# Keys projected and exponentiated two tiles ahead of their sums, with six feature buffers, in the first stage of a fused attention and mixture kernel

## Chip, core and metric

The kernel runs on one core of one Trainium2 chip. The metric is the device time of one execution in microseconds (us), the median of several runs. Five engines work side by side, each through a queue of its own in order: TensorE (PE, with its weight loads as PEld), VectorE (DVE), ScalarE (ACT), GpSimd (POOL) and SyncE (SP), which issues the DMA transfers.

## The reference

Three layers follow one another on 4 x 576 = 2304 tokens. The change touches the first, a linear attention with 8 heads of 64 and 128 random features:

```python
def phi(x):
    proj = np.einsum('bhsd,df->bhsf', x, w_phi)
    proj = proj - np.max(np.abs(proj), axis=-1, keepdims=True)
    return np.concatenate([np.exp(proj), np.exp(-proj)], axis=-1)
q_p, k_p = (phi(q), phi(k))
kv = np.einsum('bhsf,bhsd->bhfd', k_p, v)
z = np.sum(k_p, axis=2)
num = np.einsum('bhsf,bhfd->bhsd', q_p, kv)
den = np.einsum('bhsf,bhf->bhs', q_p, z)[..., None] + 1e-06
return (num / den).astype(np.float32)
```

Its result goes, as 2304 x 512, into a gated layer (RMS norm, then gate, value and output matrices with 1536 hidden units) and from there into a soft mixture of 8 experts. Everything is float32.

## The kernel before

There are three stages. The **first stage** goes over the keys in 18 tiles of 128 tokens. For each tile `Front.load` fetches the keys (256 KB) and `K.load_v` the values. `project` multiplies the keys by `w_phi` into two PSUM banks, one for the even and one for the odd heads ("hf" 0 and 1); the two halves of PE's rows take one each, four matmuls a bank, each seen as two instructions in the trace, so 8 + 8. `largest` and `less`, together `shift`, take the largest magnitude and subtract it (DVE). `exps` writes exp(x) and exp(-x) of a half into a buffer `kp` (ACT, two instructions a half). `kv` adds both halves into the sums of the batch entry on PE: `kv_of` (L439, 8 instructions a half) and `z_of` (L448, 8 a half). A batch entry ends every 4.5 tiles; then `Evac` copies its sums out and `Evac.turn` transposes them.

In iteration i of the loop the program writes: project and shift of tile i + 1, `kv` of tile i, `exps` of tile i + 1, and between these the other work of the stage. That is the conversion of nine pieces of the gated layer's weights (`conv_load`, `conv_scale`, `conv_join`, `conv_parts`: DMA, ACT, DVE, then ACT and POOL), the transposes of the sums (`fillers`) and the queries of the first 384 tokens in steps (`qsteps`, made by `Turned.steps` at the places in `TURNED0`: project, transpose and exponentiate, `attend` per pair of heads at steps 12, 15, 20 and 26 of 36, then `scale` and `out`).

The written order is not the order on an engine. A planner lays out each queue ahead of the run: among the instructions whose inputs and buffers it reckons ready, it takes the one that stands first in the program. Buffers with one tag go round: `kp` has four of 4 KB a partition, the keys' raw tiles four, `pr` (the shifted projections) three halves, the PSUM banks `P` two.

The **second stage** is the gated layer in six blocks of 384 tokens, with the conversion of the other nine weight pieces in its first block (two raw buffers, loaded from the block's start on); its SBUF tiles lie over those of the first stage and wait for them. The **third stage** is the expert matrices, loaded by DMA.

Of the kernel before, what the change touches and what calls it, by code (L numbers as in the profile page):

```python
# [7 lines left out]
F32 = mybir.dt.float32  # L8
# [8 lines left out]
NB, NH, SEQ, HD, DF = 4, 8, 576, 64, 128  # L17
# [3 lines left out]
TILES = NT // 128  # L21
# [19 lines left out]
def batch_parts(i):  # L41

    t0, parts = i * 128, []
    r = 0
    while r < 128:
        b = (t0 + r) // SEQ
        end = min(128, (b + 1) * SEQ - t0)
        parts.append((b, r, end))
        r = end
    return parts  # L50
# [14 lines left out]
def tile_kernel(ctx: ExitStack, tc: tile.TileContext, q2T, qT, kT, v, wbd, wg, wv, wo, rmsg, phi, w1, w2, consts, out):  # L65
# [3 lines left out]
    def pool(stack, name, space=None, bufs=1, side="left"):  # L69
        kw = {} if space is None else {"space": space}  # L70
        if space is None:
            kw["side"] = side
        if space is not DRAM:
            kw["reuse_waits"] = "tile"
        return stack.enter_context(tc.tile_pool(name=name, bufs=bufs, **kw))
# [73 lines left out]
    def conv_load(sp, bufs, *pools):  # L149

        key = next(conv_at, None)
        if key is not None:
            c = Conv(sp, pools[pieces.index(key) % len(pools)], key, bufs)
            c.load()
            loaded.append(c)

    def conv_scale():
        if loaded:
            convs.append(loaded.pop(0))
            convs[-1].scale()  # L160

    def conv_join():
        if convs:
            convs[-1].join()
            if convs[-1].n == 2:
                joined.append(convs.pop())

    def conv_parts():
        if joined:
            joined.pop(0).parts()  # L170
# [85 lines left out]
    class Reduced(Q):  # L256
# [25 lines left out]
        def exps(self, h):  # L282
            e = self.e[h]
            DVE.tensor_tensor(out=e[:, 1], in0=e[:, 1], in1=e[:, 0], op=ALU.subtract)
            ACT.activation(out=e[:, 0], in_=e[:, 1], func=AF.Exp)
            ACT.activation(out=e[:, 1], in_=e[:, 1], func=AF.Exp, scale=-1.0)
# [83 lines left out]
    with ExitStack() as pk:  # L370
        kx = pool(pk, "kx")
        sp = pool(pk, "spk")
# [35 lines left out]
        class K(Front):  # L408
# [2 lines left out]
                SP.dma_start(out=self.vt, in_=v[self.i].rearrange("p (h d) -> p h d", h=NH))  # L411

            def exps(self, hf):
                kp = sp.tile([128, 4, 2, DF], F32, tag="kp", name="kp", bufs=4)
                ACT.activation(out=kp[:, :, 0], in_=self.pr[hf], func=AF.Exp)
                ACT.activation(out=kp[:, :, 1], in_=self.pr[hf], func=AF.Exp, scale=-1.0)  # L416
                self.e[hf] = kp
# [75 lines left out]
        ks = [K(sp, psk, kT, i, kb if i else dict(kb, P=("misc", 3))) for i in range(TILES)]  # L493
# [13 lines left out]
        for _ in range(2):  # L507
            conv_load(sp, KCONV, sp)
        conv_scale()
        ks[0].project()  # L510
        for hf in range(2):
            ks[0].shift(hf)
            ks[0].exps(hf)
        fillers = []
        q0 = Turned(sp, psk, 0, {"misc": 3, "raw": 2, "pr": 3, "e": 2})
        qsteps = q0.steps(TURNED0[0:4], TURNED0[4:8], TURNED0[8:])
        qsteps = [[f for m, f in qsteps if m == n] for n in range(2 * TILES)]
        q0.begin()
        for i in range(TILES):
            k, kn = ks[i], ks[i + 1] if i + 1 < TILES else None  # L520
            if i + 3 < TILES:
                ks[i + 3].load()
            if i + 2 < TILES:
                ks[i + 2].load_v()
            if i % 2 and i // 2 + 2 < NPRE:
                conv_load(sp, KCONV, sp)
            parts = batch_parts(i)
            b = parts[0][0]
            ends = i * 128 + parts[0][2] == (b + 1) * SEQ

            def finish():
                ev = Evac(b)
                fillers.extend([lambda n=n: ev.turn(n) for n in range(3)])

            if len(parts) > 1:
                k.kv(parts[0])
                finish()
            if kn:
                kn.project()
                kn.shift(0)  # L540
                kn.largest(1)
                conv_join()
                kn.less(1)
            k.kv(parts[-1])
            for hf in range(2):
                if kn:
                    kn.exps(hf)
                if hf == 0 and i % 2:
                    conv_parts()
                    conv_scale()  # L550
                if fillers:
                    fillers.pop(0)()
                for f in qsteps[2 * i + hf]:
                    f()
            if ends and len(parts) == 1:
                finish()
# [47 lines left out]
    with ExitStack() as p2:  # L604
# [5 lines left out]
        sp = pool(tctx, "conv")  # L610
# [233 lines left out]
        for blk in range(NBLK):  # L844
            acc = [ps.tile([128, DM], F32, tag=f"acc{i}", name=f"acc{i}", bufs=1) for i in range(TPB)]
            qsteps, qnext = qnext or [], None
            if blk == 1:
# [6 lines left out]
                sp = pool(pctx, "post", side="right")  # L854
            if blk == NBLK - 1:
# [5 lines left out]
                sp = pool(pctx, "post", side="right")  # L861
# [62 lines left out]
    with ExitStack() as p3:  # L924
        sp = pool(p3, "sp3")
# [145 lines left out]
```

## Time and profile before

| what | value |
|---|---|
| median of 3 runs | 745.16 us (744.03 to 750.23) |
| the profiled execution's own time | 744.73 us |
| its span | 742.9 us |
| mean granted TensorE clock | 0.995 of full |
| PE busy | 713.5 us, 96% of the span |
| ACT, DVE busy | 371.6 us (50%), 428.1 us (58%) |
| first stage, from the span's start to PE's first gate matmul (L804) | 134.2 us |

The time is the execution's, the span is what the trace covers, 1.8 us less. In the trace a row gives start, duration, engine, line, operation and tile; the bracket behind it is the idle time of that engine before the row and what ended it. A busy PE is not PE at its best rate: the spacing of the rows shows how fast the same work goes.

### The profile page before, as it was taken

The page shows a single profiled execution, that of the slowest core. Times are in us where ns is not written, and L with a number is a line of the kernel's source. Part 1 is how long each engine was busy: PE and PEld are TensorE (multiplying, and loading weights), DVE is VectorE, ACT ScalarE, POOL GpSimd, SP SyncE. Part 2 cuts the span into 40 slices and gives each one's busy share as a digit, 9 for nine tenths or more (in the row PEclk, how much of TensorE's full clock was granted, in tenths as well). Part 3 has the DMA queues.
Part 4 walks back from the last instruction along what each step waited for, and adds up shares of the span by engine and source line. Part 5 has one row for each costly group of instructions (what it writes and reads, how often), then busy time and mean ns, then how long its engine had stood idle before and what let it go on. Part 6 is the DMA issues. An engine that isn't in the chain of part 4 may idle for free.

```text
span 742.9 us, 12354 instructions
## 1 busy us (share of the span) xinstructions
PE 713.5 (96%) x4919; PEld 575.1 (77%) x4919; DVE 428.1 (58%) x808; ACT 371.6 (50%) x805; POOL 108.3 (15%) x60
## 2 busy tenths in 40 slices
PE   6999898999899999999999999999999999999894
PEld 4555554888789888898888988889888899988343
DVE  5888956687756646555565555655556453323313
ACT  6689855588644465334654346543465431211103
POOL 0222210135200211012110121101211010000100
PEclk9999999999999999999999999999999999999998
DMA  9674211545010100101000010000100237657898
GB/s 325 225 243 182 72 44 45 187 158 208 8 61 23 33 22 23 49 0 33 22 23 20 1 33 22 23 19 1 33 1 2 65 120 275 228 199 288 318 362 285
DMA packets 25146, 79.47 MB, mean 107 GB/s; under 512 B 2688, under 2 KB 13376, under 8 KB 18688
## 3 DMA queue, kind: packets, MB, share of 16 engines
q1 hardware_dynamic: 24864, 77.79, 30.0%
q10 hardware_dynamic: 224, 0.88, 0.4%
q8 instruction: 39, 0.64, 0.3%
q14 instruction: 19, 0.16, 0.1%
HBM read 71.99 MB, written 6.67 MB: 106 GB/s over the span
## 4 chain that ended last, share of the span: by engine, by line
PE 76%; ACT 10%; DVE 6%; issue 2%; DMA 2%; POOL 1%; SPq 0%; DVEq 0%; ACTq 0%; POOLq 0%
PE pv L804 18%; PE pg L804 17%; PE acc L829 6%; PE acc L830 6%; PE acc L831 6%; PE num L206 4%; PE kacc L439 3%; PE den L214 2%; PE y L943 2%; ACT e L224 2%; PE kacc L448 2%; PE y L959 2%; DVE wt L137 1%; DMA wraw<-in_wg_dram 1%; ACT wt L127 1%
## 5 line engine op out<-in xcount | busy, mean ns | idle before, releaser
L804 PE MATMUL pv<-xnh,wv 128*128 128x384 f32 x576 | 151.6, 344 | 0.0
L804 PE MATMUL pg<-xnh,wg 128*128 128x384 f32 x576 | 150.2, 342 | 1.3 <-DVE t L812 1.0
L804 PEld LDWEIGHTS pg<-xnh,wg 128*128 128x128 f32 x576 | 104.7, 188 | 7.2 <-DVE t L812 1.5
L804 PEld LDWEIGHTS pv<-xnh,wv 128*128 128x128 f32 x576 | 103.2, 188 | 7.0 <-issue 6.7
L804 PE MATMUL pv<-xnl,wv 128*128 128x384 f32 x288 | 97.7, 339 | 0.0
L804 PE MATMUL pg<-xnl,wg 128*128 128x384 f32 x288 | 97.5, 338 | 0.0
L829 PE MATMUL acc<-wo,hh 128*128 128x512 f32 x216 | 88.6, 410 | 0.0
L280 POOL PARTITION_ALL_REDUCE qe<-qe x32 | 50.0, 1563 | 262.7 <-ACT qe L279 243.0
L830 PE MATMUL acc<-wo,hh 128*128 128x512 f32 x216 | 85.9, 397 | 0.0
L831 PE MATMUL acc<-wo,hl 128*128 128x512 f32 x216 | 85.4, 395 | 0.0
L102 ACT CAST hh<-t 128x384 fp32r<-128x384 f32 x72 | 36.7, 509 | 79.8 <-PE acc L830 66.1
L105 DVE TENSOR_TENSOR hl<-t,hh 128x384 fp32r<-128x384 f32 x72 | 41.3, 574 | 52.7 <-ACT hh L102 50.3
L812 DVE SCALAR_TENSOR_TENSOR t<-t,pg 128x384 f32<-128x384 f32 x72 | 39.7, 551 | 51.3 <-ACT t L811 51.2
L811 ACT ACTIVATE t<-pg 128x384 f32<-128x384 f32 x72 | 35.1, 488 | 62.5 <-PE pg L804 62.3
L224 ACT COPY qe<-qe 32x192 f32<-32x192 f32 x128 | 44.8, 350 | 31.7 <-DVE qe L219 30.4
L816 DVE TENSOR_TENSOR t<-t,pv 128x384 f32<-128x384 f32 x72 | 39.8, 552 | 30.2 <-PE pv L804 29.0
L804 PEld LDWEIGHTS pg<-xnl,wg 128*128 128x128 f32 x288 | 54.0, 188 | 0.3 <-DVE xnl L105 0.3
L804 PEld LDWEIGHTS pv<-xnl,wv 128*128 128x128 f32 x288 | 54.1, 188 | 0.1
L439 PE MATMUL kacc<-kp,vt 128*64 128x256 f32 (+1 forms) x320 | 43.8, 399 | 5.3 <-ACT kp L416 5.2
L831 PEld LDWEIGHTS acc<-wo,hl 128*128 128x128 f32 x216 | 40.6, 188 | 10.0 <-DVE hl L105 0.3
L829 PEld LDWEIGHTS acc<-wo,hh 128*128 128x128 f32 x216 | 40.7, 189 | 7.3 <-issue 0.3
L830 PEld LDWEIGHTS acc<-wo,hh 128*128 128x128 f32 x216 | 40.7, 188 | 6.4
(187 smaller groups left out, 1069.2 us busy)
## 6 DMA issues: line engine op xcount, KB each, us to landing
eu<-in_w_dram SPq DMA_DIRECT2D x32, 1024.0 KB, 6.5
wraw<-in_wg_dram SPq DMA_DIRECT2D x6, 1024.0 KB, 5.5
wraw<-in_wv_dram SPq DMA_DIRECT2D x6, 1024.0 KB, 6.6
wraw<-in_wo_dram SPq DMA_DIRECT2D x6, 1024.0 KB, 5.0
qraw<-in_qT_dram SPq DMA_DIRECT2D x32, 192.0 KB, 2.4
raw<-in_kT_dram SPq DMA_DIRECT2D x18, 256.0 KB, 3.5
vt<-in_v_dram SPq DMA_DIRECT2D x18, 256.0 KB, 2.9
out_dram<-ob SPq DMA_DIRECT2D x18, 256.0 KB, 3.4
```

What stands on the lines that cost most here:

```text
L102: ACT.copy(out=hi, in_=src)
L105: (lo_eng or POOL).tensor_tensor(out=lo, in0=src, in1=hi.bitcast(F32), op=ALU.subtract)
L224: ACT.copy(out=rd[64 * hh + 32 * r:64 * hh + 32 * r + 32, g], in_=dn[o:o + 32])
L280: POOL.partition_all_reduce(e[:, 0], e[:, 1], channels=128, reduce_op=bass_isa.ReduceOp.absmax)
L439: PE.matmul(out=kva[o0:o0 + 64, hh // 2], lhsT=self.vt[r0:r1, h], rhs=kp[r0:r1, hh].rearrange("p s f -> p (s f)"), start=first and hh < 2, ...
L804: PE.matmul(out=p, lhsT=w[:, a, c], rhs=x, start=n == 0, stop=n == 11)
L811: ACT.activation(out=t, in_=g, func=AF.Tanh, scale=0.5)
L812: DVE.scalar_tensor_tensor(out=t, in0=t, scalar=1.0, in1=g, op0=ALU.add, op1=ALU.mult)
L816: DVE.tensor_tensor(out=t, in0=t, in1=wide("v", m, xs), op=ALU.mult)
L829: PE.matmul(out=acc[i], lhsT=hh[:, s], rhs=w[:, 0], start=m == 0, stop=False)
L830: PE.matmul(out=acc[i], lhsT=hh[:, s], rhs=w[:, 1], start=False, stop=False)
L831: PE.matmul(out=acc[i], lhsT=hl[:, s], rhs=w[:, 0], start=False, stop=m == MF - 1)
```

## The change

The keys' front (project, shift, exponentiate) now runs two tiles ahead of the sums: tiles 0 and 1 before the loop, and tile i + 2 in iteration i. `kp` gets six buffers instead of four (8 KB more a partition). The keys' raw tiles are asked for four tiles ahead instead of three, tile 3 before the loop; their four buffers stay.

```diff
-                kp = sp.tile([128, 4, 2, DF], F32, tag="kp", name="kp", bufs=4)
+                kp = sp.tile([128, 4, 2, DF], F32, tag="kp", name="kp", bufs=6)
...
         conv_scale()
-        ks[0].project()
-        for hf in range(2):
-            ks[0].shift(hf)
-            ks[0].exps(hf)
+        ks[3].load()
+        for k in ks[0:2]:
+            k.project()
+            for hf in range(2):
+                k.shift(hf)
+                k.exps(hf)
...
         for i in range(TILES):
-            k, kn = ks[i], ks[i + 1] if i + 1 < TILES else None
-            if i + 3 < TILES:
-                ks[i + 3].load()
+            k, kn = ks[i], ks[i + 2] if i + 2 < TILES else None
+            if i + 4 < TILES:
+                ks[i + 4].load()
```

## Rows read from the trace of the kernel before

**Rows 1.** Chain that ended last, in order of time: start, us, what.

```profile
55.04 0.52 ACT kp L416
```

**Rows 2.** Waits from 0 to 134 us: total, times, longest, in us.

```profile
ACT kp L415 <- DVE pr L402: 16.2, 8, 5.4
...
PE kacc L439 <- ACT kp L416: 5.2, 6, 1.8
...
PE P L394 <- DVE pr L402: 1.0, 2, 0.5
```

**Rows 3.** PE's timeline: sums that waited for key features.

```profile
9.80 1.08 PE L439 MATMUL kacc<-kp,vt 128*64 128x256 f32 x8 [1.42 <-ACT kp L416]
...
77.94 1.08 PE L439 MATMUL kacc<-kp,vt 128*64 128x256 f32 x8 [0.83 <-ACT kp L416]
...
95.97 1.08 PE L439 MATMUL kacc<-kp,vt 128*64 128x256 f32 x8 [0.19 <-ACT kp L416]
...
128.47 1.08 PE L439 MATMUL kacc<-kp,vt 128*64 128x256 f32 x8 [1.79 <-ACT kp L416]
```

**Rows 4.** PE's timeline from 60 to 140 us: whole and divided groups.

```profile
86.70 1.16 PE L394 MATMUL P<-wbd_f,raw 64*128 64x128 f32 x16
87.79 1.95 PE L439 MATMUL kacc<-kp,vt 128*64 128x256 f32 x16
...
90.67 0.44 PE L337 MATMUL T<-cst,qpr 128*128 128x128 f32 x2
...
92.89 1.08 PE L439 MATMUL kacc<-kp,vt 128*64 128x256 f32 x8
...
94.65 1.13 PE L394 MATMUL P<-wbd_f,raw 64*128 64x128 f32 x8
...
97.98 0.44 PE L337 MATMUL T<-cst,qpr 128*128 128x128 f32 x2
...
117.09 3.34 PE L439 MATMUL kacc<-kp,vt 128*64 128x256 f32 x16
...
132.04 1.53 PE L476 MATMUL kvt<-cst,kvs 128*128 128x128 f32 x12
```

**Rows 5.** Timeline of the first tiles, PE's rows.

```profile
14.47 1.08 PE L439 MATMUL kacc<-kp,vt 128*64 128x256 f32 x8
...
18.04 1.13 PE L322 MATMUL P<-wbd_f,qraw 128*128 128x256 f32 x4
...
20.18 0.65 PE L439 MATMUL kacc<-kp,vt 128*64 128x256 f32 x2
...
20.76 1.16 PE L394 MATMUL P<-wbd_f,raw 64*128 64x128 f32 x8
...
21.85 1.08 PE L439 MATMUL kacc<-kp,vt 128*64 128x256 f32 x6
...
25.41 0.44 PE L337 MATMUL T<-cst,qpr 128*128 128x128 f32 x2
```

**Rows 6.** Stretches: length, PE, PEld, DVE, ACT, POOL busy, PEclk, DMA, GB/s.

```profile
70.00:80.00 10.00, 7.86 (x82) 5.08 (x84) 8.81 (x14) 10.00 (x22) 0.00 (x0) 1.00 0.30 80
...
100.00:110.00 10.00, 10.00 (x110) 5.39 (x104) 4.55 (x8) 4.52 (x10) 0.00 (x0) 1.00 0.10 26
```

**Rows 7.** The same view in stretches of 1 us.

```profile
114.00:115.00 1.00, 0.51 (x3) 0.32 (x3) 1.00 (x3) 1.00 (x3) 0.00 (x0) 1.00 0.52 197
...
118.00:119.00 1.00, 1.00 (x8) 0.56 (x6) 1.00 (x5) 0.00 (x0) 0.00 (x0) 0.50 0.00 0
```

**Rows 8.** Waits of SP's DMA queue from 0 to 134 us.

```profile
SPq L123 <- PE kvt L476: 17.6, 1, 17.6
```

**Rows 9.** PE's timeline in the second stage's first block: its waits.

```profile
188.16 0.62 PE L804 MATMUL pg<-xnh,wg 128*128 128x384 f32 x2 [1.05 <-DVE t L812]
...
197.20 0.87 PE L206 MATMUL num<-e,kv 128*64 128x192 f32 x8 [1.20 <-ACT e L339]
```

**Rows 10.** Groups by line from 0 to 260 us: busy, mean ns.

```profile
L415 ACT ACTIVATE kp<-pr 128x512 f32<-128x512 f32 x36 | 22.9, 635 | 19.6 <-DVE pr L402 16.2 <-DVE rs L182 3.3
```

## The prediction

> **What bounds the kernel now.** I read the chain that ended last first, to see which engine carries the first stage, where the whole change lies. Up to about 96 us it runs mostly over ACT, DVE and POOL, with the key exponentials among its links [rows 1]; behind that it is PE. The waits of the stage come next [rows 2]: PE's sums waited 5.2 us in all, six times, for a key exponential on ACT, and PE's projections 1.0 us, twice, for a PSUM bank that the subtraction on DVE still held. Third, PE's own timeline [rows 3], for where these waits lie: 1.42 us before the first tile, a few around 72 to 80 us, and 1.79 us before the last tile's sums. Last, the spacing of PE's rows, because a busy PE is not PE at its best [rows 4]. The sums of tile 11, with the projection of tile 12 ahead of them, show the whole groups: sixteen projection matmuls take 87.79 - 86.70 = 1.09 us, and the sums of a tile 90.67 - 87.79 = 2.88 us. The last tile's sums, for which the planner had the second half of the features late, are divided into halves and take 132.04 - 128.47 = 3.57 us [rows 3, 4]. So a late feature costs twice: as a wait, and as a half group in which the array's two halves, or its four strips, don't all work.
>
> How full are the other engines? From 70 to 80 us ACT is busy 10.00 of 10 us, DVE 8.81, PE only 7.86; from 100 to 110 us, with the weight conversion over, ACT and DVE are below half [rows 6]. The middle of the stage is ACT's, its end PE's.
>
> **The change part by part.**
>
> *Features one iteration earlier.* The number of instructions stays; a tile's four exponentials (4 x 0.635 = 2.5 us of ACT [rows 10]) move ahead of one iteration's other work on ACT (conversion, query steps), and its reductions and subtractions likewise on DVE; these are what now queues behind them, and the query steps' transposes and `attend` on PE wait for that. Sums of tile i no longer need what ACT did just before. Gain, waits: 5.2 - 1.42 = 3.8 us; the first wait stays, since tile 0 must still be loaded, projected, shifted and exponentiated before anything can be summed. Of the 3.8 us, 1.79 lies at the end [rows 3], where ACT is idle for more than half of the time [rows 6]: kept whole. The rest, 5.2 - 1.42 - 1.79 - 0.19 = 1.8 us, lies between 72 and 80 us (one of these waits is shown [rows 3]), where ACT is full; a tile in hand covers it, but ACT must have built that tile up earlier, out of what slack it has in the stage's first part, and what PE no longer waits for here it may wait for at the next query step. I count half of it, 0.9 us, as lost. Net 2.9 us; bounds 1.8 (only the end) and 3.8.
>
> *Divided sums.* Against 2.88 us whole [rows 4], tile 17 loses 0.69 us; tile 12 takes (94.65 - 92.89) + (97.98 - 95.97) = 3.77 us [rows 3, 4], a loss of 0.89; tile 1 takes 18.04 - 14.47 = 3.57, a loss of 0.69, and tile 2 (20.76 - 20.18) + (25.41 - 21.85) = 4.14, a loss of 1.26 [rows 5]. With both halves ready an iteration before, the planner has no reason to divide the late two: 1.58 us. Tiles 1 and 2 come while DVE is still building the lead, so I take half of 1.95 us, 0.98. Together 2.6 us; bounds 0 and 3.5.
>
> *Two tiles before the loop.* Tile 1's projection already stands directly behind tile 0's in the queues, so the start is laid out as before: no gain, no loss, from -0.5 to +0.5 us by the size of one projection (1.09).
>
> *Raw tiles four ahead.* Each load waits for one of four buffers that the projection of four tiles before has to free; that is the limit before and after. Moving the request in the program past a value load, and tile 3 past two query loads at the start, changes no wait that PE shows: the only one of its waits for a key load is that for tile 0. Zero.
>
> *Six feature buffers.* If feature buffers were scarce, ACT's exponentials would wait for PE's sums to release one. The rows show ACT waiting before them 16.2 us, but for DVE's subtraction [rows 2], and no such wait for a release. So the two buffers alone are worth nothing; they only allow the new order. The Trainium skill says otherwise at first reading: Perfetto Trace Analysis, section Identifying the Most-Contended Engine, takes a bubble that repeats on the busiest engine as a sign that SBUF or PSUM is short for the next tile. By that rule the 3.8 us would be the buffers' and would come whatever the order; the trace's releasers speak against it, and the sum stays the same.
>
> The buffers have a second effect. By the sizes of the tiles in the code, everything allocated behind `kp` in the stage moves up by 8 KB. The second stage's first raw weight buffer lay over the copies of the sums (`kvs`), so its load had to wait in SP's queue until the last transposes, 17.6 us [rows 8]. It will lie over query features, which are read for the last time before the last tiles' sums. The block behind it has only two PE waits, 1.05 and 1.20 us [rows 9], so an earlier conversion is worth 0 to 2.25 us. I take 0, because the second raw buffer then still lies over the copies and the conversion needs both.
>
> *Clock.* Between 118 and 119 us the granted clock is 0.50, the 1.2 GHz level, after a microsecond with PE busy for only 0.51 [rows 7]; the group of sums there takes 3.34 instead of 1.95 us [rows 4]. PE's slack just before was a wait for a PSUM bank [rows 2], behind the last `attend`, and the change puts another tile's projection at the same place. I take 0; bounds 0 and 1.4 us gained. The Trainium skill (TensorE: Matmul & The Clock Gate, part 1) has the clock fall after idleness of PE; by it less waiting would keep the 2.4 GHz level here, and the sum would be 1.4 us lower. What fell away here, though, is not the wait that came before the fall.
>
> **Sum.** 2.9 + 2.6 = 5.5 us. Behind the first stage everything starts as much earlier: block after block PE follows without pause, and the loads of the second stage are released by the first stage's end. The profiled execution took 744.73 us, 1.8 more than its span and 0.43 less than the median, so 739.2 on its own scale, and 745.16 - 5.5 = 739.7 by the median. I write 739.5.
>
> **The rivals.**
>
> *All of it comes.* Waits 3.8, divisions 3.5, the clock 1.4 and half of the first block's waits 1.1: 9.8 us, so 735. For it: each is visible in rows. Against it: they would all have to go, in a stretch where ACT is full.
>
> *ACT keeps the pace.* If ACT cannot build up a tile in hand before the middle, its order merely changes: exponentials first, query steps 2.5 us later, and PE waits at transposes and `attend` for what it waited for at the sums. Then only the end is gained, 1.8 + 0.7 = 2.5 us, and 0.5 to 1 us lost at the steps: 743. For it: [rows 1, 6]. Against it: before the first weight pieces have landed ACT has little but the keys' features to do.
>
> *Divided projections, on the slow side.* Tile i + 2's projection stands ahead of tile i's sums in the program, and the planner takes it as soon as one of the two `P` banks is free. Eight matmuls of one half take 21.85 - 20.76 = 1.09 us [rows 5], as long as sixteen of both (1.09 [rows 4]): a projection cut in the middle costs 1.09 us more. A PE that no longer waits for features comes to the banks sooner after DVE's first subtraction, and finds one free and one not. If ten of the projections now whole are cut, that is 10.9 us against the 2.9 + 2.6 gained: 750. It decides from six cuts on. For it: the banks are the tightest buffers of the stage, and their waits show [rows 2]. Against it: the sums and projections keep their order in the program, and PE has a whole tile of ready sums to do while a bank is still held.
>
> *It does nothing*, because the planner's queues already ran as far ahead as buffers allowed: 745. Against it: features that arrived only just [rows 3] show they didn't.
>
> **How the numbers follow.** Chances: forecast 0.50 (736.5 to 742.5), all of it 0.20 (732 to 737), ACT's pace or no effect 0.20 (742 to 746), divided projections 0.10 (746 to 753). The likeliest gives 739.5. For 8 in 10 I leave out a tenth at each end: 734 to 746.5. One per cent, about what a measurement of this kernel can tell from no change, is 7.5 us: faster means below 737.7, slower above 752.6. Faster: a quarter of the forecast's 0.50 and nearly all of the 0.20, 0.31. Slower: the tail of the last case, 0.04. Same: 0.65.
>
> **What the changed profile would show.** Right: no sum waits for `kp` except at the start; sums in runs of sixteen, 2.88 us a tile, the last one directly behind the one before; projection 17 ahead of the sums of tile 15; PE's first gate matmul near 128.7 us instead of 134.2; the first raw weight load of the second stage issued before the last transposes. Wrong: ACT or DVE steps of the queries as new releasers of PE between 50 and 100 us; projections in eights in most tiles; or `out` of the queries arriving after PE is ready for the gate. Also wrong would be a first stage that ends sooner while the first block's conversion ends no earlier, so that PE waits there instead.

## The result and the profile after

| | before | after |
|---|---|---|
| median of 6 runs each | 745.36 us (744.03 to 750.23) | 739.52 us (736.88 to 741.87) |
| ratio to before, 95% interval | | 0.9911 [0.9891, 0.9931] |
| the profiled execution, its span | 744.73, 742.9 us | 736.88, 735.0 us |
| PE's first gate matmul | 134.23 us | 128.05 us |
| the same less PE's wait for the first key tile | 129.63 us | 124.18 us |

The kernel became 5.8 us faster by the medians, 0.9%: inside the forecast, and less than the one per cent that the prediction calls faster. The profiled execution after is the fastest of its six and shows 7.9 us. Its parts, from the traces: 0.73 us because the first key tile landed earlier (not shown to be the change's doing: in the profiled executions of the kernels below this landing varies from 3.9 to 4.8 us), 5.45 us in the rest of the first stage, 0.9 us in the first block of the second, and 0.8 us spread behind it.

Lines behind the loop have moved by two (L804 is L806 now). PE's waits up to 130 us, as total, times and longest, answer to [rows 2]:

```profile
PE P L394 <- DMA raw<-in_kT_dram: 3.9, 1, 3.9
PE P L322 <- ACT xraw L216: 1.9, 1, 1.9
PE P L322 <- DVE kv L485: 1.7, 2, 1.3
PE kacc L439 <- ACT kp L416: 1.7, 2, 1.2
PE P L394 <- DVE pr L402: 0.8, 2, 0.5
```

The sums' wait for key features fell from 5.2 to 1.7 us, of which 1.16 is the first tile's. A wait of 1.9 us is new (it was 0.15): a query projection waits until ACT has copied `xraw` out of the bank it needs. PE's timeline at the end of the stage, against the 1.79 us wait of the last tile there [rows 3]:

```profile
114.72 0.94 PE L394 MATMUL P<-wbd_f,raw 64*128 64x128 f32 x12
115.59 1.95 PE L439 MATMUL kacc<-kp,vt 128*64 128x256 f32 x16
...
118.47 1.08 PE L439 MATMUL kacc<-kp,vt 128*64 128x256 f32 x6
119.70 0.91 PE L347 MATMUL r<-dg,small 128*128 128x384 f32 x2 [0.15 <-DVE dg L246]
120.54 1.51 PE L439 MATMUL kacc<-kp,vt 128*64 128x256 f32 x10
...
122.98 1.95 PE L439 MATMUL kacc<-kp,vt 128*64 128x256 f32 x16
...
125.86 1.53 PE L476 MATMUL kvt<-cst,kvs 128*128 128x128 f32 x12
...
128.05 0.62 PE L806 MATMUL pg<-xnh,wg 128*128 128x384 f32 x2 [0.23 <-ACT xnh L102]
```

The last projection (it ends at 115.59) stands ahead of the sums of tile 15; the sums of tile 17 follow those of tile 16 without a pause and are whole: 125.86 - 122.98 = 2.88 us.

Where did the stage's time go? I add up the distance from each PE row's start to the next one's, less the idle time in the bracket, by operation, up to the first gate matmul:

| | before | after |
|---|---|---|
| sums, L439 | 41.8 us | 43.0 us |
| sums, L448 | 23.5 us | 21.1 us |
| key projections, L394 | 27.8 us | 26.2 us |
| PE's other work | 27.7 us | 27.3 us |
| PE's waits (with the first load) | 13.5 us | 10.4 us |

So 3.1 us of the gain is the same work done in less time, and 2.4 us is waiting (3.1, less the 0.73 of the first load). The two kinds of sums together fell by 1.2 us only, L448's less by 2.4 and L439's more by 1.2; the key projections fell by 1.6. Either stage holds one stretch at half clock, worth 1.7 us each (a stretch's length times what the granted clock lacks of 1.00): before, between 117 and 121 us [rows 7]; after, from 65.9 to 69.3 us, 1.3 us behind the end of the new wait. Stretches of 1 us, columns as in [rows 6]:

```profile
63.00:64.00 1.00, 0.00 (x0) 0.00 (x0) 1.00 (x3) 1.00 (x3) 0.00 (x0) 1.00 0.00 0
64.00:65.00 1.00, 0.35 (x2) 0.30 (x2) 1.00 (x2) 1.00 (x3) 0.00 (x0) 1.00 0.00 0
65.00:66.00 1.00, 1.00 (x13) 0.72 (x12) 1.00 (x4) 1.00 (x2) 0.00 (x0) 0.94 0.00 0
66.00:67.00 1.00, 1.00 (x8) 0.78 (x8) 1.00 (x2) 1.00 (x2) 0.36 (x1) 0.50 0.00 0
```

Why the new wait? ACT's timeline after, just before it:

```profile
61.63 0.63 ACT L415 ACTIVATE kp<-pr 128x512 f32<-128x512 f32 x1
62.16 0.61 ACT L416 ACTIVATE kp<-pr 128x512 f32<-128x512 f32 x1
...
63.10 0.61 ACT L415 ACTIVATE kp<-pr 128x512 f32<-128x512 f32 x1
63.62 0.61 ACT L416 ACTIVATE kp<-pr 128x512 f32<-128x512 f32 x1
64.14 0.46 ACT L216 COPY xraw<-num 128x384 f32<-128x384 f32 x1
```

The copy of the second `attend`'s result stands behind two pairs of key exponentials, 4 x 0.53 = 2.1 us of a full ACT, and PE stood still for 1.94 us until it was done. The exponentials that PE used to wait for are now ahead of what PE waits for instead.

The first raw weight load of the second stage, which had waited 17.6 us for the last transposes [rows 8], is released by something earlier, and in that stage's first block one of PE's two waits [rows 9] shrank. From after, SP's queue and PE's timeline:

```profile
SPq L123 <- PE r L347: 6.1, 1, 6.1
```

```profile
181.07 0.62 PE L806 MATMUL pg<-xnh,wg 128*128 128x384 f32 x2 [0.39 <-DVE t L814]
...
190.10 0.87 PE L206 MATMUL num<-e,kv 128*64 128x192 f32 x8 [1.19 <-ACT e L339]
```

From the first gate matmul to the second of these rows it is 62.05 us, where it was 62.97.

### The profile page after: what moved, and what is told of

Its sections match the earlier page's. It is cut to its first block, busy times and chain, and to the rows that moved or that the text cites. A ratio compares the mean times of both kernels' runs of the same rounds, so it can differ in the third digit from the quotient of the medians.

```text
span 735.0 us, 12347 instructions
## 1 busy us (share of the span) xinstructions
PE 710.2 (97%) x4919; PEld 575.0 (78%) x4919; DVE 429.5 (58%) x808; ACT 371.8 (51%) x805; POOL 107.9 (15%) x60
## 3 DMA queue, kind: packets, MB, share of 16 engines
q1 hardware_dynamic: 24864, 77.79, 30.2%
## 4 chain that ended last, share of the span: by engine, by line
PE 79%; DVE 9%; ACT 7%; issue 2%; POOL 1%; DMA 1%; SPq 0%; DVEq 0%; ACTq 0%; POOLq 0%
PE pv L806 20%; PE pg L806 19%; PE acc L831 6%; PE acc L832 6%; PE acc L833 6%; PE num L206 4%; PE kacc L439 2%; PE den L214 2%; ACT e L224 2%; PE y L945 2%; DVE wt L139 2%; PE y L961 2%; DVE wt L137 2%; PE P L394 1%; PE kacc L448 1%
## 5 line engine op out<-in xcount | busy, mean ns | idle before, releaser
L806 PE MATMUL pv<-xnh,wv 128*128 128x384 f32 x576 | 151.5, 344 | 0.0
L806 PE MATMUL pg<-xnh,wg 128*128 128x384 f32 x576 | 150.2, 342 | 0.6 <-DVE t L814 0.4
L806 PEld LDWEIGHTS pg<-xnh,wg 128*128 128x128 f32 x576 | 104.7, 188 | 6.3 <-ACT xnh L102 0.6
L806 PEld LDWEIGHTS pv<-xnh,wv 128*128 128x128 f32 x576 | 103.2, 188 | 7.0 <-issue 6.7
L806 PE MATMUL pv<-xnl,wv 128*128 128x384 f32 x288 | 97.7, 339 | 0.0
L806 PE MATMUL pg<-xnl,wg 128*128 128x384 f32 x288 | 97.5, 338 | 0.0
L806 PEld LDWEIGHTS pg<-xnl,wg 128*128 128x128 f32 x288 | 54.0, 188 | 0.3 <-DVE xnl L105 0.3
L806 PEld LDWEIGHTS pv<-xnl,wv 128*128 128x128 f32 x288 | 54.1, 188 | 0.1
L439 PE MATMUL kacc<-kp,vt 128*64 128x256 f32 (+1 forms) x320 | 44.8, 396 | 1.7 <-ACT kp L416 1.7
```

What stands on the lines that cost most here:

```text
L439: PE.matmul(out=kva[o0:o0 + 64, hh // 2], lhsT=self.vt[r0:r1, h], rhs=kp[r0:r1, hh].rearrange("p s f -> p (s f)"), start=first and hh < 2, ...
L806: PE.matmul(out=p, lhsT=w[:, a, c], rhs=x, start=n == 0, stop=n == 11)
```

## The experiments

My theory after the result: the order is what gains, by features in hand and by whole groups of matmuls; and part of it is given back where ACT is full. The rivals: the buffers gain (as rooms for what PE waits for, or by moving the second stage's tiles); or the end of the stage gains everything. Each kernel is compared with runs of the kernel before on the same chip; "stage" is the time of the first gate matmul less the wait for the first key tile (129.63 before, 124.18 after), from one profiled execution.

The stage also holds the clock. In six of these executions (e2, e4, e5, e6, e7 and e10) the sums of tile 0 run at about half speed, where the others, before and after among them, have them at full speed. From e6, against the rows of before [rows 3] and of after (9.07, in the part on the steps of the prediction):

```profile
9.25 1.97 PE L439 MATMUL kacc<-kp,vt 128*64 128x256 f32 x8 [1.42 <-ACT kp L416]
11.15 1.06 PE L448 MATMUL kacc<-kp,small 128*32 128x256 f32 x2
```

Eight sums take 1.9 us instead of 1.0. The clock's column shows 1.00 there, but the first record of the clock in these six traces lies at 12.3 to 13.4 us, behind these rows, and in the others at 7.0 to 8.9, ahead of them; so I read it as the 1.2 GHz level lasting longer at the start. The column "at full clock" is my estimate of the stage without either loss: 1.7 us off for each spell at half clock in it, and 1.4 to 1.9 us, by the spacing of tile 0's rows, for such a start. On this scale before is 127.9 and after 122.5, a gain of 5.4.

| experiment | ratio to before, 95% interval | median, beside before's | stage | at full clock |
|---|---|---|---|---|
| e8_change_again | 0.9913 [0.9881, 0.9944] | 739.90 / 746.53 | 124.2 | 122.4 |
| e1_six_buffers | 1.0010 [0.9993, 1.0027] | 746.82 / 745.85 | 129.6 | 127.9 |
| e2_loads_four | 1.0009 [0.9986, 1.0032] | 747.21 / 745.85 | 129.4 | 128.1 |
| e3_lead2_four_buffers | 0.9966 [0.9941, 0.9990] | 742.40 / 745.85 | 126.4 | 126.4 |
| e4_lead3 | 0.9942 [0.9922, 0.9962] | 741.79 / 745.85 | 126.8 | 123.7 |
| e5_lead2_late | 0.9974 [0.9957, 0.9991] | 744.76 / 746.01 | 128.3 | 125.1 |
| e6_lead2_early | 1.0023 [1.0003, 1.0043] | 748.38 / 746.01 | 132.1 | 126.9 |
| e7_queries_first | 0.9946 [0.9925, 0.9967] | 742.25 / 746.01 | 127.8 | 122.9 |
| e9_attend_later | 0.9913 [0.9881, 0.9945] | 741.13 / 746.53 | 126.0 | 124.3 |
| e10_divided_sums | 0.9999 [0.9977, 1.0021] | 747.00 / 746.53 | 132.2 | 130.4 |
| e11_divided_projections | 1.0008 [0.9981, 1.0035] | 746.94 / 746.53 | 130.9 | 129.2 |
| e12_whole_projections | 1.0024 [0.9996, 1.0052] | 747.00 / 745.12 | 131.0 | 127.6 |

A time also holds the spells at half clock, which differ between executions of one kernel by up to some 3 us (last section); a difference of a few tenths of a per cent therefore decides nothing by itself, and I read the stage and its waits with it. Nor are these spells spread evenly over the kernels: of the 35 runs of before beside e1 to e4, 22 have a mean granted clock of 0.994 or more; of the 12 runs each of e1, e4, e5, e6 and e12, none has.

### The parts alone: buffers, loads, order

**e1_six_buffers**: the kernel before with the buffers alone.

```diff
-                kp = sp.tile([128, 4, 2, DF], F32, tag="kp", name="kp", bufs=4)
+                kp = sp.tile([128, 4, 2, DF], F32, tag="kp", name="kp", bufs=6)
```

> The kernel before with six feature buffers and nothing else. Theory (the order pays, by removing PE's waits for features and its divided groups): the order in the program stays, no exponential waited for a buffer, so the time stays within 1 us of the kernel before, PE's sums wait about 5 us for features as before, and only the second stage's first raw weight load is issued some 10 us earlier. Rival (buffers were short): most of the 5.8 us comes here. Rival (the shift of the SBUF tiles pays): 1 to 2 us faster, in the second stage's first block alone.

Same time, the same stage with the same spell at half clock, the same 5.2 us of waiting for `kp`: buffers without the order are worth nothing in the stage. What the shift of the tiles does to the second stage shows behind it. The same two rows in this kernel, whose first gate matmul is at 134.00:

```profile
187.25 0.62 PE L804 MATMUL pg<-xnh,wg 128*128 128x384 f32 x2 [0.57 <-DVE t L812]
...
196.29 0.87 PE L206 MATMUL num<-e,kv 128*64 128x192 f32 x8 [1.19 <-ACT e L339]
```

62.29 us, and half of the first wait gone. So the earlier load is worth some 0.7 us here. The time doesn't show it: in the profiled execution the clock also fell at the expert matrices, and all twelve runs have a mean clock of 0.988 to 0.990, where most of before's have 0.995.

**e2_loads_four**: the kernel before with the loads alone.

```diff
+        ks[3].load()
...
-            if i + 3 < TILES:
-                ks[i + 3].load()
+            if i + 4 < TILES:
+                ks[i + 4].load()
```

> The kernel before with the keys asked for four tiles ahead, tile 3 before the loop, and nothing else. Theory: the four raw buffers set when a load can go, so the time stays within 1 us of the kernel before and the first stage ends at 134 us. Rival (the early loads pay): some of the 5.8 us comes here, with key loads issued earlier from the first iterations on.

Same time, same waits: nothing, as forecast. The stage agrees for a reason that the sum hides: it has no spell at half clock, but the slow start; without both it is 128.1 against 127.9.

**e3_lead2_four_buffers**: the change without its buffers.

```diff
-                kp = sp.tile([128, 4, 2, DF], F32, tag="kp", name="kp", bufs=6)
+                kp = sp.tile([128, 4, 2, DF], F32, tag="kp", name="kp", bufs=4)
```

> The changed kernel with four feature buffers. Theory (order, not room): projection and shift run two tiles ahead, the exponentials of tile i + 2 can start as soon as the sums of tile i release their buffers, which is still most of a tile ahead of need, so at least two thirds of the gain stay: 739.5 to 741.5 us. Rival (the third tile's buffers are what lets ACT work ahead): the gain is gone, 744 to 746 us, with ACT waiting for PE's sums before its exponentials and PE for the features after.

Less than I expected: 0.34 of the 0.87 to 0.89 per cent, four tenths by the time (the interval reaches from a tenth to two thirds). Of the stage's 3.2 us, 1.7 is a spell at half clock that this execution didn't have; at full clock the order alone gains 1.5 of 5.4 us. PE's waits here, and one of ACT's:

```profile
PE P L322 <- ACT xraw L216: 2.5, 1, 2.5
PE P L322 <- DVE kv L485: 2.5, 2, 1.3
PE kacc L439 <- ACT kp L416: 2.0, 2, 1.5
```

```profile
ACT kp L415 <- PE kacc L448: 8.0, 4, 2.6
```

The wait for features is gone as in the changed kernel; what came back is larger at the query steps. The exponentials of two tiles ahead need a buffer that older sums must free: ACT waited 8.0 us for that, four times, and in neither before nor after is there such a wait. That the query steps, behind the exponentials in ACT's and DVE's order, are late because of it fits the larger waits, but is argued. So the order is necessary (e1) but not enough; room for it carries the rest. The second stage's rows are as before, 194.49 - 131.17 = 63.3 us from gate to `num`: with four buffers its tiles don't move, which confirms e1's reading of the 0.7 to 0.9 us.

**e4_lead3**: three tiles ahead, with eight buffers.

```diff
...
-        for k in ks[0:2]:
+        for k in ks[0:3]:
...
-            k, kn = ks[i], ks[i + 2] if i + 2 < TILES else None
+            k, kn = ks[i], ks[i + 3] if i + 3 < TILES else None
```

> The changed kernel with the front three tiles ahead and eight buffers. Theory: PE's waits for features are already down to 1.7 us in the changed kernel, 1.16 of it before the first tile, so at most 0.5 us is left to gain, while ACT's query steps fall back by another 2.5 us of exponentials: 738 to 742 us, no faster than the changed kernel by more than 0.5 us. Rival (more lead, more gain): another 3 us or more, 736 us or below.

No more, by the stage 2.6 us less (1.2 at full clock). The feature wait is the first tile's alone (1.4 us), but PE waits 2.3 us for `kv L485`, 1.2 us for `xraw`, and 1.7 us before sums for something that the trace doesn't name. A second tile in hand buys nothing that one doesn't.

### Where in the stage: late or early

**e5_lead2_late** keeps one tile ahead until iteration 8, where tile 9 is built in addition; **e6_lead2_early** stays two ahead until iteration 8 and falls back to one.

```diff
...
-            k, kn = ks[i], ks[i + 2] if i + 2 < TILES else None
+            lead = 1 if i < 8 else 2
+            k, kn = ks[i], ks[i + lead] if i + lead < TILES else None
+            if i == 8:
+                ks[9].project()
...
```

```diff
-            k, kn = ks[i], ks[i + 2] if i + 2 < TILES else None
+            lead = 2 if i < 8 else 1
+            k, kn = ks[i], ks[i + lead] if i + lead < TILES and i != 8 else None
```

> One tile ahead for the first eight iterations, a second tile made up in iteration 8, two ahead from there; six buffers, loads as in the changed kernel. Theory: the waits between 72 and 80 us, the divided sums of tiles 12 and 17 and the 1.79 us before tile 17 lie behind it, so half to two thirds of the gain comes: 741 to 742.5 us; but the tile must be made up where ACT is full. Rival (the gain is made in the first tiles, by whole projections and sums): 744 us or more.

> Two tiles ahead for the first eight iterations, one ahead from iteration 8 on; six buffers, loads as in the changed kernel. Theory: the waits and divided sums near the end come back (1.79 us and 0.69 us before and in tile 17), a third of the gain stays: 742.5 to 744 us. Rival (the gain is made in the first tiles): 740 us or less.

Both fell short in time. Late: PE's only wait for features left is the first, 1.4 us, and still the stage gains only 1.3 us, 2.8 at full clock: the tile has to be built up in the middle, where ACT is full, and its projections are cut more (L394 takes 28.6 us, 26.2 after). Its time, 744.76 us, lies where the rival put it, which the next kernel contradicts. Early: slower than before, with the `xraw` wait and the feature waits both (2.0 and 4.5 us, 1.7 of these before tile 17 as in before), two spells at half clock and the slow start; at full clock its stage still gains about 1.0 us. So neither the first tiles nor the end alone makes the gain, and the parts, 2.8 and 1.0, don't add up to the change's 5.4: the rest, as I read it, comes of a lead that is built early and kept to the end. That a lead given up half way gains nothing isn't shown; its loss in time goes with a clock that was lower in all twelve runs (0.983 to 0.989).

### The new wait

**e7_queries_first**: in an iteration, the exponentials behind the query steps in the program instead of ahead of them.

```diff
-                if kn:
-                    kn.exps(hf)
...
+                if kn:
+                    kn.exps(hf)
```

> The changed kernel with the key exponentials of tile i + 2 written behind the other work of the iteration (conversion, transposes of the sums, query steps) instead of ahead of it. Theory: in the changed kernel PE waited 1.94 us at 64.65 us for the copy of a query sum that stood behind two pairs of exponentials on ACT, and its clock fell behind that wait (about 1.75 us); with a tile in hand the exponentials can come last, so both go: 735.5 to 738 us. Rival (ACT is simply full there): PE waits for features instead, 739 to 742 us.

It didn't do what I meant: the planner still put two pairs of exponentials before that copy, the `xraw` wait is 1.9 us as in the changed kernel, features are later (2.6 us of waits instead of 1.7), and the stage holds a second spell at half clock and the slow start; at full clock it is within 0.4 us of the changed kernel's. So it doesn't test the wait's price.

**e8_change_again**: no edit; is the wait, and the spell at half clock behind it, the queue's or the execution's?

> The changed kernel once more, beside the next three on one chip. Theory: 739 to 740 us. Its trace shows whether the fall of the clock at 65 us is the kernel's or that execution's: if the wait of 1.94 us decides, the granted clock is 0.50 for some microseconds behind it again; if not, the same wait stands there at full clock.

The queue's, as far as two executions show: 1.93 us and a spell at 66 to 70 us again, stage 124.2.

**e9_attend_later**: the second `attend` two steps later.

```diff
-TURNED0 = [2, 8, 14, 20, 12, 15, 20, 26, 28, 31]
+TURNED0 = [2, 8, 14, 20, 12, 17, 20, 26, 28, 31]
```

> The changed kernel with the second attend of the queries at step 17 instead of 15, so one iteration later. Theory (the exponentials and copies of the first attend hold up the second one's copy on ACT): the 1.94 us wait at 64.65 us goes, and with it the clock's fall where there is one: 2 to 3.5 us faster than the changed kernel, 736 to 738 us. Rival (ACT is full and PE waits at another step): 739 to 741 us.

The wait moved to another releaser, ACT's `e L339` (2.0 us, with 0.7 left of `xraw`), and the time stayed within its interval; the profiled execution's stage is 1.9 us longer than the changed kernel's. That fits a full ACT: in the stretch from 60 to 80 us it is busy for 19.8 of 20 us after. What the wait costs by itself I could not take out; that it is the price of the order in a full ACT is supported by e7 and e9, not proved.

### What a divided group costs

The rival on the slow side stood on this price, so I measured it. **e10_divided_sums** writes the sums of a tile half by half, and **e11_divided_projections** the projections, so that the planner keeps them apart.

```diff
-                for f in (self.kv_of, self.z_of):
-                    for hf in range(2):
-                        f(hf, part)
+                self.kv_of(0, part)
+                self.z_of(0, part, range(1))
+                self.kv_of(1, part)
+                self.z_of(0, part, range(1, 4))
+                self.z_of(1, part)
...
```

> The changed kernel with every tile's sums written in the order in which the planner divided them: eight of the first half, one strip of the ones-sum, eight of the second half, the rest. The work is the same. Theory (a divided sum costs 0.69 us): of 20 parts some 18 are newly divided, 12 us more, 751 to 753 us, with PE's rows at 3.57 us a part instead of 2.88. Rival (the price is hidden, because PE waits elsewhere for less): below 744 us.

PE's timeline, one tile:

```profile
91.50 1.08 PE L441 MATMUL kacc<-kp,vt 128*64 128x256 f32 x8
92.52 0.62 PE L450 MATMUL kacc<-kp,small 128*32 128x256 f32 x2
93.07 1.08 PE L441 MATMUL kacc<-kp,vt 128*64 128x256 f32 x8
94.08 1.06 PE L450 MATMUL kacc<-kp,small 128*32 128x256 f32 x14
95.08 0.44 PE L337 MATMUL T<-cst,qpr 128*128 128x128 f32 x2
```

3.58 us instead of 2.88: the sums lose 0.15 us (1.02 + 1.01 instead of 1.88), but the two instructions of a single strip take 0.55 where sixteen over all strips take 1.0, and the fourteen that are left still take 1.0. L450 rose from 21.1 to 30.2 us and the sums of L441 by 2.4, together 11.5 of the 12 us expected; the waits fell from 10.9 to 8.0. The kernel is 7.1 us slower than the changed one beside it (747.00 against 739.90), between the theory's time and the rival's.

```diff
-                for c in range(4):
-                    for hf in range(2):
+                for hf in range(2):
+                    for c in range(4):
```

> The changed kernel with each key projection written half by half, eight instructions for one PSUM bank and then eight for the other. The work is the same. Theory (half of the array's rows stands idle, 1.09 us a tile): some 12 projections that were whole cost 1.09 us more, 13 us, 751 to 754 us. Rival (PE reaches the second bank sooner or later anyway; DVE can start on the first bank earlier, so part comes back): 740 to 746 us.

L394 rose from 25.9 to 35.0 us, the waits without the first load fell from 6.8 to 5.1, and the kernel is 7.0 us slower than the changed one, here too between theory and rival. So the price in the prediction was real, 9.1 us (13 expected) for projections divided throughout, of which about a fifth comes back as waits that are gone. Both orders end where the kernel before is: dividing either kind of group throughout costs about as much as the whole change gains.

**e12_whole_projections** goes the other way: what if no projection were cut?

```diff
-                self.p = [self.ps.tile([128, 4, DF], F32, tag=tag, name="P", bufs=n) for _ in range(2)]
+                if tag == "misc":
+                    self.p = [self.ps.tile([128, 4, DF], F32, tag=tag, name="P", bufs=n) for _ in range(2)]
+                else:
+                    both = self.ps.tile([128, 2, 4, DF], F32, tag=tag, name="P", bufs=1)
+                    self.p = [both[:, hf] for hf in range(2)]
```

> The changed kernel with the two halves of a key projection taken together: both accumulators lie in one tile of two banks, so a projection can begin only when VectorE has read both of the one before, and its sixteen matmuls are then queued in pairs that share a place instead of eight of one half and later eight of the other (tile 0 keeps its own). Theory (what is left of the divided groups still costs: 26 us of projection rows stand in the first stage of the changed kernel, and eighteen whole projections at 1.09 would be 19.6): the rows of L394 fall to 20 to 21 us and most of that reaches the first gate matmul, 735 to 737.5 us. Rival (the one shared accumulator makes PE wait until VectorE has read the last half): PE waits for pr by 4 to 8 us more and nothing is gained, 739 to 743 us, or slower.

The rival's case. L394 did fall, from 26 to 22.0 us, but PE waited 6.9 us, three times, before projections. The waits of this kernel, and PE's and DVE's timelines at the longest of them (L398 is the projection here, L402 and L406 are `largest` and `less`):

```profile
PE P L398 <- issue: 6.9, 3, 3.5
```

```profile
72.60 1.16 PE L398 MATMUL P<-wbd_f,raw 64*128 64x128 f32 x16 [3.55 <-issue]
```

```profile
70.48 0.56 DVE L225 TENSOR_TENSOR xraw<-xraw,e 128x384 f32<-128x384 f32 x1 [4.68 <-ACT e L224]
70.95 0.68 DVE L402 TENSOR_REDUCE mx<-P 128x4 f32<-128x512 f32 x1
...
71.82 0.68 DVE L406 TENSOR_TENSOR pr<-P,mx 128x512 f32<-128x512 f32 x1
```

The trace names no releaser, but the projection starts 0.1 us after DVE's subtraction has read the second bank (71.82 + 0.68 = 72.50), and so it does at the other long wait, of 3.02 us (27.32 behind 26.55 + 0.68 = 27.23). DVE itself stood 4.68 us in a query step waiting for ACT, with the reduction and subtraction of that half queued behind. In the changed kernel PE would meanwhile have filled the bank that was free. The cut projection is the price of that, and here it is the cheaper of the two. The bank isn't the whole of the loss: the sums of L452 (L448 in the changed kernel) rose from 21.1 to 24.5 us, and the stage holds a second spell at half clock. The Trainium skill (Perfetto Trace Analysis, section Optimizing Tensor Performance) asks that independent groups of matmuls go round through different PSUM banks, so that one bank is read while the next is filled; this run agrees with it, 747.0 us and 1.0024 of before with the two banks tied together, where the changed kernel has 0.9911.

## Why the prediction was right, step by step

*Features one iteration earlier* (2.9 us, bounds 1.8 to 3.8). Measured: waits for `kp` less by 3.6, of which 0.26 is the first tile's, so 3.3 of the 3.8; waits elsewhere more by 1.2 net (`xraw` +1.8, `kv` +0.35, `dg` +0.15, against `qpr` -0.9 and `pr` -0.2). Net 2.4. The mechanism, one wait taking the place of another where ACT is full, came as written, at the `attend` of a query pair, and a little larger than the 0.9 us allowed: a part of the rival "ACT keeps the pace" came true.

*Divided sums* (2.6 us). Measured 3.1 us in the spacing of PE's rows, but the sums hold only 1.2 of it; 1.6 lies in the key projections, which the sum had no gain for. That the total came out near is luck. The last tile gave its 0.69 us as said, but tile 16, whole before, is now cut by `r` (L347) and takes (119.70 - 0.15 - 118.47) + (122.98 - 120.54) = 3.52 us, a loss of 0.64 (lines in the section on the result). Tile 12 was to come whole and is still cut, so it gave 0.3 of its 0.89. PE's rows of it after:

```profile
92.47 0.65 PE L439 MATMUL kacc<-kp,vt 128*64 128x256 f32 x2
...
94.44 1.94 PE L439 MATMUL kacc<-kp,vt 128*64 128x256 f32 x14
...
97.31 0.44 PE L337 MATMUL T<-cst,qpr 128*128 128x128 f32 x2
```

The fourteen and what follows take 2.87 us, as long as a whole tile, so the two ahead of them are all loss, some 0.6 us. Two steps failed, then: "With both halves ready an iteration before, the planner has no reason to divide the late two", for tile 12, and "Tiles 1 and 2 come while DVE is still building the lead, so I take half of 1.95 us". Tiles 0 to 2 took 3.58 + 3.57 + 4.14 = 11.3 us before and 4.14 + 4.14 + 3.45 = 11.7 us after: nothing came back there, as tile 0 and tile 1 are cut more. PE's rows of these two after:

```profile
9.07 1.08 PE L439 MATMUL kacc<-kp,vt 128*64 128x256 f32 x8 [1.16 <-ACT kp L416]
...
11.21 1.17 PE L394 MATMUL P<-wbd_f,raw 64*128 64x128 f32 x16
12.31 1.08 PE L439 MATMUL kacc<-kp,vt 128*64 128x256 f32 x6
...
14.31 1.08 PE L439 MATMUL kacc<-kp,vt 128*64 128x256 f32 x8
...
16.88 1.17 PE L394 MATMUL P<-wbd_f,raw 64*128 64x128 f32 x16
17.98 0.65 PE L439 MATMUL kacc<-kp,vt 128*64 128x256 f32 x2
...
19.55 1.13 PE L322 MATMUL P<-wbd_f,qraw 128*128 128x256 f32 x4
```

(Tile 0 from 9.07 to 14.31, tile 1 from there to 19.55, a projection of 1.10 us inside each.) What I had left out made up for it: the projections themselves are cut less, 1.6 us. Over the whole stage L448 takes 2.4 us less, as much as four or five divided tiles (0.55 us each, e10), but L439 1.2 us more, as its runs are cut elsewhere.

*Two tiles before the loop* (0, from -0.5 to +0.5). The start is not laid out as before: the projections of the tiles to come now stand inside the sums of tiles 0 and 1, which is the 0.4 us just counted.

*Raw tiles four ahead* (0): right within the noise, e2.

*Six buffers* (0 alone): right in the stage, e1. But "they only allow the new order" was too weak: without them the order keeps four tenths by the time, three by the stage at full clock (e3). The Trainium skill's rule on a bubble that repeats (Perfetto Trace Analysis; it stands in the section Optimization Strategy, right behind the one that the prediction names: too little SBUF or PSUM for the next tile) was weighed in the prediction and set aside. For the kernel before that stands, 1.001 with the buffers alone; for the kernel with the new order the rule would have been the better guide (ACT's 8.0 us of waits for a release in e3). The shift of the tiles was taken as 0 because the second raw buffer still lies over the copies; the bound held, the value didn't: 0.7 to 0.9 us, since the first buffer alone lets the block's conversion start sooner (e1 with it, e3 without).

*Clock* (0, bounds 0 to 1.4). One spell of 1.7 us fell away and another of 1.7 us came. The sum was right, and by chance.

*Rivals.* Divided projections: the price is real (e11), the case didn't come, since the number of cuts went down, not up. All of it comes: not, because of ACT. The signs named (the last sums directly behind those before, projection 17 ahead of tile 15's sums, the raw load before the last transposes) all came; the gate matmul at 128.05 instead of 128.7 is the first load's 0.73. Two others did not: one sum behind the start still waits for `kp` (0.5 us), and the sums of tiles 0 to 3, 9, 10, 12 and 16 are not whole. And one sign of being wrong came, a query step on ACT as a new releaser of PE, the `xraw` wait at 64.65 us; it is the part that this account gives to the rival.

## What to carry to other kernels

A wait that a lead takes away from the bottleneck's inputs can come back at whatever stands behind the advanced work on the producer's queue (here 1.2 of 3.6 us); count the producer's slack stage by stage, and keep a lead once it is built, since here its two halves alone gave about 2.8 and 1.0 of 5.4 us at full clock. Price the order with its room: alone the one gave some three tenths and the other nothing. And where the array is used in halves or strips, compare the spacing of whole and cut groups before counting waits: here PE's rows held the larger half of the gain. And take the clock out before comparing stages: here that changed what several experiments say.

## What the runs showed that I had not expected

**The granted clock depends on more than the last wait.** From 106 us on e2 has the same PE rows as before, 0.4 us later, waits for the same `pr` just as long (0.50 us, at 115.37), has a microsecond there with PE busy for only 0.63 (before 0.51 [rows 7]; here the wait lies across two of them), and yet kept the 2.4 GHz level where before fell to 1.2. Nor does the new wait bring its spell by itself: e3 stood 2.5 us for `xraw` and e9 2.0 us for `e L339`, with no spell behind either. Stretches of e2:

```profile
115.00:116.00 1.00, 0.63 (x4) 0.47 (x4) 0.94 (x3) 1.00 (x4) 0.00 (x0) 1.00 0.08 29
118.00:119.00 1.00, 1.00 (x12) 0.66 (x10) 1.00 (x4) 0.00 (x0) 0.00 (x0) 1.00 0.09 33
```

**The same queue can meet it or not.** How often differs by kernel, as the experiments' runs show, and why is open. The first expert matrices, 128 matmuls each, in the changed kernel and in its repeat e8 (durations in ns as least, median and most, then first and last start):

```profile
L945 PE MATMUL y<-eu,xo x128: 592/592/617, 689.1 to 703.8; 128*32 128x512 f32 x128
```

```profile
L945 PE MATMUL y<-eu,xo x128: 592/593/1063, 690.2 to 706.8; 128*32 128x512 f32 x128
```

PE has the same gaps ahead of them in both, in a chain over DVE and ACT. The same microsecond of each, and then a later one of e8 alone:

```profile
684.00:685.00 1.00, 0.38 (x3) 0.08 (x1) 0.49 (x2) 0.17 (x1) 0.00 (x0) 1.00 1.00 426
```

```profile
684.00:685.00 1.00, 0.38 (x5) 0.11 (x2) 0.50 (x2) 0.00 (x0) 0.00 (x0) 1.00 0.97 410
...
687.00:688.00 1.00, 0.90 (x7) 0.50 (x5) 0.71 (x2) 0.24 (x1) 0.00 (x0) 0.70 0.99 418
```

In e8 the clock stood at half until 694 us, and the group took 1.9 us longer; in the other execution it stayed full. With the 1.1 us by which it began later, this is the 3.0 us between the two spans, 735.0 and 738.0. The Trainium skill (TensorE: Matmul & The Clock Gate, part 1) says that the moment at which the clock is decided is not tied to the kernel's start and varies from run to run; this pair agrees. In this case it makes the profiled execution after look about 2 us better than the medians say.
